# Scoring tokens against code words in quarters of 32, eight groups to a score bank, in a residual quantizer

## The chip, the cores and the metric

The kernel runs on one core of one Trainium2 chip. The metric is the device time of one execution in microseconds (us). Three runs of the kernel before gave 798.52, 801.80 and 803.55 us; their median, 801.8 us, is the time before.

The profile names the engines PE (TensorE, matmuls; PEld is its weight load), DVE (VectorE), ACT (ScalarE), POOL (GpSimd) and SP (SyncE, which issues transfers here).

## The reference

A small audio codec: a depthwise filter of three taps along time, SiLU, four stages of residual vector quantization with eight code words each, and a second depthwise filter over the sum of the chosen words.

```python
B, T, D, K = 2, 16000, 512, 3
Nq, C = 4, 8

z = zeros_like(x)
for i in range(K):
    z = z + xp[:, i:i+T, :] * dw_enc[i][None, None, :]
z = silu(z)
res, q = z, zeros_like(z)
for s in range(Nq):
    cb = codebooks[s]
    d2 = einsum("btd,btd->bt", res, res)[..., None] - 2.0 * einsum("btd,cd->btc", res, cb) + einsum("cd,cd->c", cb, cb)[None, None, :]
    idx = d2.argmin(-1)
    sel = cb[idx]
    q = q + sel
    res = res - sel
y = zeros_like(x)
for i in range(K):
    y = y + qp[:, i:i+T, :] * dw_dec[i][None, None, :]
return y
```

`xp` and `qp` are x and q with one row of zeros ahead of and behind each sequence. All arrays are bf16. The squared norm of the residual is part of each distance, so it has to be computed for every token and stage.

## The kernel before

**Layout.** The 32,000 tokens are 250 groups of 128: partition p holds 250 successive tokens, and group g is the token g of every partition. The 512 features are four blocks (index i) of 128, features on partitions. The groups are cut into 17 chunks (`SIZES`: 4, 12, fourteen of 16, 10). A chunk that is no multiple of four is padded, so the last one is worked on as 12.

**Front of a chunk** (`load`, `front`). The first two chunks come in as rows and are turned by TensorE; the others come through transposing transfers on SP's queue (L361), one for each group and two for the neighbours. Then for each feature block: three products with the taps on VectorE (L415); their sum, one addition by an accumulating transfer on POOL's queue (L421) and one on VectorE (L423), in the first two chunks both on VectorE; SiLU as exp (ScalarE, L427), plus one (VectorE, L431), log (ScalarE, L435), exp (ScalarE, L438), and the product with z (VectorE, L443), which writes the residual tile `RES`.

**RES.** One of three buffers, 128 x 4 blocks x 32 halves x 96 columns. A half is 64 tokens, with 16 columns of code words (times -2) ahead of it and 16 behind it. `code_columns` (L221, L222) writes these columns once in each buffer.

**A stage** (`stage`, four for each chunk). `score` fills a PSUM bank with up to `GB` = 6 groups: a matmul of the identity with `MASK` (L494) puts 0 on the diagonal and a huge negative number beside it; then, for each group, feature block and half of 64 tokens, a matmul (L499) has the 64 tokens as weights, and as moving operand the same 64 tokens with the code words that lie beside them as far as this stage needs: 80 columns in the first and last stage, 72 in the others. The diagonal of the 64 x 64 part is the squared norm; the mask lets a maximum over the row find it. `norm` (L507, VectorE) takes that maximum over 64 columns a group, `dots` (L510, VectorE) copies the eight products with code words. A chunk of 16 has three banks a stage, of 6, 5 and 5 groups; two banks exist. Six small instructions on VectorE (L527 to L554) make the one-hot choice, TensorE turns it (L564), ScalarE copies it out (L571).

Then the chosen words are subtracted from RES, for each feature block i and each pair of quarters of the chunk (j = 0 and 2). Blocks with i below `on_dve[s]` go over VectorE: TensorE puts the words in PSUM (L589, SEL) and VectorE adds (L604). The other blocks go over ScalarE: TensorE adds RES and words in PSUM (L610 and L589, NEW) and ScalarE copies back (L615). `ON_DVE` gives two blocks to VectorE in each of the three stages that subtract; its second row holds for the last chunk alone (`LAST` = 1). The last stage subtracts nothing.

**Output** (`finish`, `outputs`). The decoder's taps are multiplied into the code words at the start, so each output group is a sum of two matmuls on the turned one-hot choices (L640); ScalarE copies pairs of groups out (L646) into one of `YB` = 3 buffers, and SP stores four groups at a time.

**The order.** Nothing is placed by hand: `Plan` holds every step with an engine, a cost (hold and delay), what it needs and a due time, plays the engines forward with these costs, and at each point gives a free engine the ready step with the earliest due. The order that comes out is the program's. Buffers are counted as slots in it (`ZB`, `TB`, `EB`, `LNB`, `YB`, three RES buffers, two score banks `psG`, three `psA`). `LEAD`, `STAGE`, `LATE` and `SPREAD` set the dues in units of `PERIOD`: a block of a chunk's front is due at its chunk's origin plus (i x SPREAD - LEAD) periods, stage s at s x STAGE, the output at 3 x STAGE + LATE. Where the plan finds TensorE little used in its last 3.4 us, `warm` puts in a matmul that nobody reads (L316), to keep the engine's clock up.

Of the kernel before, what the change touches and what calls it, by code (L numbers as in the profile page):

```python
# [10 lines left out]
BF16 = mybir.dt.bfloat16  # L11
F32 = mybir.dt.float32
ALU = mybir.AluOpType
ACT = mybir.ActivationFunctionType
AX = mybir.AxisListType
# [2 lines left out]

GC = 16
J = 4  # L20
GB = 6
HT = 64
LC = 16

SIZES = [4, 12] + [16] * 14 + [10]


ON_DVE = ((2, 2, 2), (2, 3, 3))
LAST = 1

WARM = 0.5

DMA_ADDS = 1
DMA_MORE = 0

ZB, TB, EB, LNB, YB = 4, 5, 2, 1, 3
PERIOD, LEAD, STAGE, LATE, SPREAD = 48, 0.6, 0.7, 1.2, 0.2
FAR = -3.3e38


# [80 lines left out]
def kernel(  # L121
# [8 lines left out]
    nc = tc.nc  # L130
    P = nc.NUM_PARTITIONS
    B, T, D = x.shape
    K = dw_enc.shape[0]
    Nq, C, _ = codebooks.shape
    KT = D // P
    S = B * T // P
    NC = Nq * C
    HB = P // B
    assert K == 3 and D % P == 0 and B * T % P == 0 and P % B == 0 and J * NC == P and Nq * C == 32


    xf = x.flatten_outer_dims()
# [2 lines left out]
    const = ctx.enter_context(tc.tile_pool(name="const", bufs=1))  # L145
# [8 lines left out]
    psG = ctx.enter_context(tc.tile_pool(name="psG", bufs=2, space=bass.MemoryType.PSUM))  # L154
# [27 lines left out]
    for i in range(KT):  # L182
# [1 line left out]
    nc.vector.tensor_copy(WENC, psw[:, 0:4 * KT].rearrange("p (i k) -> p i k", k=4)[:, :, 0:K])  # L184

    free = {"RES": [], "KEY": [], "OH": []}
    plan = Plan({"XT": 2, "Z": ZB, "T": TB, "E": EB, "LN": LNB, "Y": YB, "psG": 2, "psA": 3, "RES": 3, "KEY": 3,
                 "OH": 3})

    RESB = []  # L190
    for n in range(3):
        t = const.tile([P, KT, 2 * GC, NC + HT], BF16, name=f"RES{n}")
        RESB.append(t)
        free["RES"].append(t)

# [1 line left out]

    xv = xf.rearrange("(p g) d -> p g d", g=S)
    G, G2 = chunks[0]["G"], chunks[0]["G"] + chunks[1]["G"]
    XR = RESB[2].rearrange("p k h c -> p (k h c)")[:, 0:(G2 + 2) * D].rearrange("p (g d) -> p g d", d=D)  # L200
    nc.vector.memset(XR[0:1, 0, :], 0.0)
    nc.vector.memset(XR[HB:HB + 1, 0, :], 0.0)
    nc.sync.dma_start(out=XR[:, 1:G + 2, :], in_=xv[:, 0:G + 1, :])
# [14 lines left out]
                                scalar2=None, op0=ALU.mult)  # L218

    def code_columns(t):  # L220
        nc.vector.tensor_copy(t[:, :, :, 0:LC], CBT[:, :, :, 0:LC].to_broadcast([P, KT, 2 * GC, LC]))  # L221
        nc.vector.tensor_copy(t[:, :, :, LC + HT:], CBT[:, :, :, LC:].to_broadcast([P, KT, 2 * GC, LC]))  # L222


    GPOS = const.tile([P, NC], BF16, name="GPOS")
# [16 lines left out]
        nc.vector.tensor_copy(GPOS, psg[:, 0, 0:NC])  # L242


    MASK = const.tile([P, GB, HT], BF16, name="MASK")

    def mask():
        for h in range(2):
            for r in range(GB):
                nc.vector.tensor_scalar(out=MASK[h * HT:(h + 1) * HT, r, :], in0=IDENT[h * HT:(h + 1) * HT, h * HT:(h + 1) * HT],  # L250
                                        scalar1=-1.0, scalar2=-FAR, op0=ALU.add, op1=ALU.mult)


    CBN = [const.tile([P, D], BF16, name=f"CBN{s}") for s in range(Nq - 1)]
# [41 lines left out]
    early = -4.0 * PERIOD  # L296
    words_in = plan.add("WORDS", 3.5, 3.5, [], early, lambda: None)
    codes = [plan.add("DVE", 0.3, 0.5, [words_in], early, code_words)]
    codes[0] = plan.add("DVE", 1.2, 1.4, codes, early + 2.0, lambda: code_columns(RESB[0]))
    scored = [plan.add("DVE", 2.4, 2.6, [], early + 1.0, mask), plan.add("DVE", 1.9, 2.1, [words_in], early + 1.0, code_norms)]  # L300
    preset = [plan.add("DVE", 0.8, 1.0, [], early + 2.0 if n == 0 else 0.1 * PERIOD, lambda n=n: presets(n)) for n in range(3)]
    words = plan.add("DVE", 1.0, 1.2, [words_in], early + 3.0, stage_words)
    codes.append(plan.add("DVE", 1.2, 1.4, [codes[0]], 0.1 * PERIOD, lambda: code_columns(RESB[1])))
    decoder = []
    for n, name in enumerate(PARTS):
        t = plan.add("DVE", 0.2, 6.0, [], (0.3 + 0.02 * n) * PERIOD, lambda name=name: taps_of(name))
# [14 lines left out]
    def load_rows(st, org):  # L321
        G, g0 = st["G"], st["g0"]
        moved = []

        def room():
            st["XT"] = xpool.tile([P, KT, GC + 2, P], BF16, name="XT")

        def turn(i):
            pst = psA.tile([P, 2, 512], F32, name="ps_x", tag="psa")
            st["ps", i] = pst.rearrange("p b n -> p (b n)").bitcast(BF16)  # L330
            for n in range(G + 2):
                nc.tensor.transpose(st["ps", i][:, n * P:(n + 1) * P], XR[:, g0 + n, i * P:(i + 1) * P], IDENT)

        def move(i):
            src = st["ps", i][:, 0:(G + 2) * P].rearrange("p (n t) -> p n t", t=P)
            if i % 2:
                nc.vector.tensor_copy(st["XT"][:, i, 0:G + 2, :], src)
            else:
                nc.scalar.activation(st["XT"][:, i, 0:G + 2, :], src, ACT.Copy)

        rows = plan.add("ROWS", 0.1 + 0.9 * G, 0.1 + 0.9 * G, [], early + org, room, take=("XT",))
        for i in range(KT):
            t = plan.add("PE", 0.12 * (G + 2), 0.12 * (G + 2) + 0.2, [rows], early + org, lambda i=i: turn(i),
                         take=("psA",))
            moved.append(plan.add(("ACT", "DVE")[i % 2], (0.11, 0.07)[i % 2] * (G + 2), (0.11, 0.07)[i % 2] * (G + 2) + 0.2, [t],
                                  early + org, lambda i=i: move(i), give=("psA",)))
        st["loaded"] = moved
        if g0:
            codes.append(plan.add("DVE", 1.2, 1.4, moved + codes[0:1], early + org + 1.0, lambda: code_columns(RESB[2])))

    def load(st, org):
        g0, G, GP = st["g0"], st["G"], st["GP"]
# [33 lines left out]
    def front(st, org):  # L386
# [14 lines left out]
        def places(t):  # L401
            return t[:, 0:G, :].rearrange("p (j m) t -> p j m t", m=MB)

        def halves(t):
            return t[:, 0:G, :].rearrange("p n (h t) -> p (n h) t", t=HT)

        def block(i):
            u = {}
# [31 lines left out]
            def silu():  # L440
                if i == 0:
                    st["RES"] = free["RES"].pop(0)
                nc.vector.tensor_tensor(out=st["RES"][:, i, 0:2 * G, LC:LC + HT], in0=halves(u["Z"]), in1=halves(u["E"]),  # L443
                                        op=ALU.mult)

            due = org + (i * SPREAD - LEAD) * PERIOD

# [26 lines left out]
    def stage(st, s, due):  # L474
# [4 lines left out]
        u = {}  # L479
        seen, maxima = [], []  # L480


        lo, hi = (min(C * s, LC), LC + HT) if C * s < LC else (LC, LC + HT + C * (s + 1) - LC)
        own = LC - lo
        pick = 0 if C * s < LC else hi - lo - C

        def score(q, m):
            RES = st["RES"]
            if q == 0:
                u["TR"] = small.tile([P, GC], BF16, name="TR")  # L490
                u["PR"] = small.tile([P, GC, C], BF16, name="PR")
            PS = pending.pop() if pending else psG.tile([P, 512], F32, name="PS")
            V = u["V", q] = PS[:, 0:m * (hi - lo)].rearrange("p (r c) -> p r c", r=m)
            nc.tensor.matmul(V[:, :, own:own + HT], lhsT=IDENT, rhs=MASK[:, 0:m, :], start=True, stop=False, skip_group_check=True)  # L494
            for r in range(m):
                for i in range(KT):
                    for h in range(2):
                        half = RES[:, i, 2 * (q + r) + h, :]
                        nc.tensor.matmul(V[h * HT:(h + 1) * HT, r, :], lhsT=half[:, LC:LC + HT], rhs=half[:, lo:hi],  # L499
                                         start=False, stop=(i == KT - 1), skip_group_check=True)  # L500
            if s == Nq - 1 and q + m == G:
                free["RES"].append(RES)
            if not scored[2:]:
                scored.append(None)

        def norm(q, m):
            nc.vector.tensor_reduce(out=u["TR"][:, q:q + m], in_=u["V", q][:, :, own:own + HT], axis=AX.X, op=ALU.max)  # L507

        def dots(q, m):
            nc.vector.tensor_copy(u["PR"][:, q:q + m, :], u["V", q][:, :, pick:pick + C])  # L510

        banks = -(-G // GB)
        q = 0
        for n in range(banks):
            m = -(-(G - q) // (banks - n))
            needs = [st["new"][i, j] for i in range(KT) for j in range(q // MB, (q + m - 1) // MB + 1)]
            needs += scored[0:2] + ([codes[st["n"]]] if st["n"] < 3 else [])
            t = plan.add("PE", 0.05 + 0.25 * m, 0.25 + 0.25 * m, needs, due, lambda q=q, m=m: score(q, m), take=("psG",),
                         give=("RES",) if s == Nq - 1 and q + m == G else (), use=0.7)
            seen.append(t)  # L520
            maxima.append(plan.add("DVE", 0.07 + 0.065 * m, 0.2 + 0.065 * m, [t], due, lambda q=q, m=m: norm(q, m)))
            maxima.append(plan.add("DVE", 0.06 + 0.01 * m, 0.2, [maxima[-1]], due, lambda q=q, m=m: dots(q, m), give=("psG",)))
            q += m

# [65 lines left out]
                             skip_group_check=True)  # L590

        def tokens(i, j, count):
            return st["RES"][:, i, 2 * j * MB:2 * (j + count) * MB, LC:LC + HT]

        def pair(i, j):
            return tokens(i, j, 2).rearrange("p (h m) t -> p h m t", h=2)

        def chosen(i, j):
            u["SEL", i, j] = psA.tile([P, 2, 512], F32, name="SEL", tag="psa")
# [2 lines left out]

        def subtract(i, j):
            nc.vector.tensor_tensor(out=pair(i, j), in0=pair(i, j), op=ALU.add,  # L604
                                    in1=u["SEL", i, j][:, :, 0:W].rearrange("p h (m t) -> p h m t", t=HT))

        def rest(i, j):
            NEW = u["NEW", i, j] = psA.tile([P, 2, 512], F32, name="NEW", tag="psa")
# [3 lines left out]
                select(NEW[:, h, 0:W], i, j + h, False)  # L612

        def keep(i, j):
            nc.scalar.activation(pair(i, j), u["NEW", i, j][:, :, 0:W].rearrange("p h (m t) -> p h m t", t=HT), ACT.Copy)  # L615

        due += 0.01 * PERIOD
        for j in range(0, J, 2):
# [122 lines left out]
```

## Time and profile before

| | |
|---|---|
| median of three runs | 801.8 us |
| the profiled execution, its own time | 801.33 us |
| its span, first to last instruction | 799.5 us |
| busy: DVE, ACT, PE, PEld, POOL | 733.6, 677.3, 654.2, 321.9, 62.8 us |
| granted TensorE clock, mean | 0.935 |
| L604 subtraction on VectorE | 208 instructions, 228.7 us |
| L615 subtraction on ScalarE | 200 instructions, 187.8 us |
| L499 score matmuls | 8064 instructions |
| L507 maxima on VectorE | 188 instructions, 94.4 us |
| L427, L435, L438 on ScalarE | 68 instructions each, 122.3, 122.3 and 122.4 us |
| L646 output copies on ScalarE | 126 instructions, 124.9 us |

In the profile L with a number is a line of the kernel; `out<-in` are tile names; a matmul's `128*64` is the weights' rows and columns. A row's mean is from an instruction's start to its end, and on one engine the next instruction may start before that end; the busy time of an engine counts overlapped time once. Idle time ahead of a group is given with what ended it. The busy time of PE holds pipelined matmuls whose ends are modelled.

### The profile page before, as it was taken

Reading aid. Unit: us, or ns where it says so; the run is one execution under the profiler, and the core shown is the slowest. Engines: PE = TensorE matmul, PEld = TensorE weight load, DVE = VectorE, ACT = ScalarE, POOL = GpSimd, SP = SyncE. Lnnn points to the kernel's source line nnn. Section 1 sums busy time; section 2 is a strip of 40 time slices with the busy share of each in tenths; the row PEclk is TensorE's granted clock in tenths of the full one; section 3 lists DMA queues with packets and bytes.
Section 4 is the critical chain, followed back from the end, with each engine's and each line's share of the span. In section 5 each row is a group of like instructions: output and inputs, shape, how many; then the busy total and the mean of one; then the engine's idle time right before and its main releaser. Section 6 shows DMA issues by size and latency. Waiting matters only on the chain.

```text
span 799.5 us, 23767 instructions
## 1 busy us (share of the span) xinstructions
PE 654.2 (82%) x10454; PEld 321.9 (40%) x10454; DVE 733.6 (92%) x1494; ACT 677.3 (85%) x603; POOL 62.8 (8%) x77
## 2 busy tenths in 40 slices
PE   1585878888888888878888798988888888889996
PEld 1333344433434443533444354444344443534443
DVE  5899799999999999999999999999999999968772
ACT  1567949799799998999998999989989998996666
POOL 0202010100001000000010100010000111000000
PEclk9987889999999998998999998999989999979999
DMA  7408595568676676799683997659767745120224
GB/s 185 81 16 147 110 146 104 97 130 167 129 132 154 116 156 134 121 186 192 133 148 67 216 143 158 121 102 206 163 136 147 142 89 146 33 88 3 107 107 184
DMA packets 162816, 102.77 MB, mean 129 GB/s; under 512 B 146201, under 2 KB 146586, under 8 KB 162586
## 3 DMA queue, kind: packets, MB, share of 16 engines
q1 hardware_dynamic: 153252, 69.77, 39.6%
q0 software_dynamic: 9312, 31.37, 22.5%
q8 instruction: 81, 1.33, 0.7%
q14 instruction: 21, 0.17, 0.1%
q10 hardware_dynamic: 150, 0.13, 0.1%
HBM read 2.92 MB, written 32.77 MB: 45 GB/s over the span
## 4 chain that ended last, share of the span: by engine, by line
DVE 55%; ACT 18%; PE 18%; DMA 5%; issue 2%; SPq 0%; POOL 0%; ACTq 0%; DVEq 0%
DVE RES L604 17%; DVE T L415 7%; DVE Z L423 6%; DVE TR L507 6%; DVE RES L443 5%; ACT YSB L646 5%; PE PS L499 4%; PE NEW L610 4%; ACT RES L615 4%; DVE Z L415 3%; ACT E L427 3%; ACT LN L435 3%; DVE E L431 3%; PE Y L640 3%; ACT E L438 3%
## 5 line engine op out<-in xcount | busy, mean ns | idle before, releaser
L604 DVE TENSOR_TENSOR RES<-RES,SEL 128x1024 bf16<-128x1024 bf16 (+2 forms) x208 | 228.7, 1128 | 12.5 <-PE SEL L589 12.2
L615 ACT ACTIVATE RES<-NEW 128x1024 bf16<-128x1024 f32 (+2 forms) x200 | 187.8, 976 | 58.1 <-PE NEW L589 54.4
L499 PE MATMUL PS<-RES 128*64 128x80 bf16 (+1 forms) x8064 | 185.1, 206 | 23.3 <-DVE RES L443 18.9
L499 PEld LDWEIGHTS <-RES 128*64 128x64 bf16 x8064 | 161.2, 117 | 67.1 <-issue 32.2
L610 PE MATMUL NEW<-RES,IDENT 128*128 128x512 bf16 (+2 forms) x400 | 124.9, 397 | 39.9 <-ACT RES L615 14.6
L427 ACT ACTIVATE E<-Z 128x2048 bf16<-128x2048 bf16 (+2 forms) x68 | 122.3, 1802 | 22.4 <-DVE Z L423 22.3
L435 ACT ACTIVATE LN<-E 128x2048 f32<-128x2048 bf16 (+2 forms) x68 | 122.3, 1798 | 10.4 <-DVE E L431 10.1
L646 ACT ACTIVATE YSB<-Y 128x1024 bf16<-128x1024 f32 (+1 forms) x126 | 124.9, 1035 | 5.9 <-PE Y L640 4.8
L438 ACT ACTIVATE E<-LN 128x2048 bf16<-128x2048 f32 (+2 forms) x68 | 122.4, 1800 | 0.3
L507 DVE TENSOR_REDUCE TR<-PS 128x6 bf16<-128x384 f32 (+2 forms) x188 | 94.4, 505 | 23.6 <-PE PS L499 23.6
L421 POOL DMA_DIRECT2D Z<-T x60 | 56.0, 933 | 607.9 <-DVE T L415 105.6
L589 PEld LDWEIGHTS <-CBN 32*128 32x128 bf16 x816 | 37.7, 92 | 158.4 <-issue 153.8
L589 PE MATMUL SEL<-OHT,CBN 32*128 32x512 bf16 (+2 forms) x416 | 73.2, 382 | 33.7 <-ACT OHT L571 13.6
L415 DVE TENSOR_SCALAR T<-XT,WENC 128x2048 bf16<-128x2048 bf16 (+2 forms) x136 | 94.4, 702 | 0.0
L640 PE MATMUL Y<-A,OHT 128*128 128x512 bf16 x249 | 82.5, 385 | 7.4 <-ACT YSB L646 6.1
L316 PE MATMUL PS<-CB,IDENT 128*128 128x512 bf16 x269 | 85.5, 435 | 2.8 <-DVE PR L510 2.8
L423 DVE TENSOR_TENSOR Z<-Z,T 128x2048 bf16<-128x2048 bf16 (+2 forms) x76 | 82.6, 1086 | 1.0 <-DMA Z<-T 1.0
L589 PE MATMUL NEW<-OHT,CBN 32*128 32x512 bf16 (+2 forms) x400 | 80.0, 396 | 0.0
L443 DVE TENSOR_TENSOR RES<-Z,E 128x2048 bf16<-128x2048 bf16 (+2 forms) x68 | 77.0, 1133 | 0.6 <-ACT E L438 0.6
L494 PE MATMUL PS<-MASK,IDENT 128*128 128x384 bf16 (+2 forms) x188 | 61.7, 328 | 10.2 <-DVE PR L510 9.8
L610 PEld LDWEIGHTS <-IDENT 128*128 128x128 bf16 x400 | 30.6, 100 | 84.9 <-issue 78.8
L640 PEld LDWEIGHTS <-OHT 128*128 128x128 bf16 x373 | 32.3, 99 | 40.9 <-issue 12.7
(74 smaller groups left out, 453.1 us busy)
## 6 DMA issues: line engine op xcount, KB each, us to landing
out_dram<-YSB SPq DMA_DIRECT2D x61, 512.0 KB, 3.2
Z<-T POOLq DMA_DIRECT2D x56, 512.0 KB, 5.7
XT<-in_x_dram SPq DMA_TRANSPOSE x263, 4.4
RES<-in_x_dram SPq DMA_DIRECT2D x1, 1536.0 KB, 10.0
Z<-T POOLq DMA_DIRECT2D x4, 384.0 KB, 6.0
RES<-in_x_dram SPq DMA_DIRECT2D x1, 640.0 KB, 6.3
out_dram<-YSB SPq DMA_DIRECT2D x1, 384.0 KB
out_dram<-YSB SPq DMA_DIRECT2D x1, 256.0 KB, 4.4
```

The lines of the kernel that those rows point to most:

```text
L415: nc.vector.tensor_scalar(out=places(u[name]), in0=taps(i, k), scalar1=WENC[:, i, k:k + 1], scalar2=None, op0=ALU.mult)
L427: nc.scalar.activation(u["E"][:, 0:G, :], u["Z"][:, 0:G, :], ACT.Exp, scale=-1.0)
L435: nc.scalar.activation(u["LN"][:, 0:G, :], u["E"][:, 0:G, :], ACT.Ln)
L438: nc.scalar.activation(u["E"][:, 0:G, :], u["LN"][:, 0:G, :], ACT.Exp, scale=-1.0)
L499: nc.tensor.matmul(V[h * HT:(h + 1) * HT, r, :], lhsT=half[:, LC:LC + HT], rhs=half[:, lo:hi], start=False, stop=(i == KT - 1), skip_group ...
L507: nc.vector.tensor_reduce(out=u["TR"][:, q:q + m], in_=u["V", q][:, :, own:own + HT], axis=AX.X, op=ALU.max)
L589: nc.tensor.matmul(ps, lhsT=CBN[s][rows, i * P:(i + 1) * P], rhs=u["OHT"][rows, 0:MB, :], start=start, stop=True, skip_group_check=True)
L604: nc.vector.tensor_tensor(out=pair(i, j), in0=pair(i, j), op=ALU.add, in1=u["SEL", i, j][:, :, 0:W].rearrange("p h (m t) -> p h m t", t=HT))
L610: nc.tensor.matmul(NEW[:, h, 0:W], lhsT=IDENT, rhs=tokens(i, j + h, 1), start=True, stop=False, skip_group_check=True)
L615: nc.scalar.activation(pair(i, j), u["NEW", i, j][:, :, 0:W].rearrange("p h (m t) -> p h m t", t=HT), ACT.Copy)
L640: nc.tensor.matmul(Y[:, h, :], lhsT=lhs(), rhs=rhs, start=(a == 0), stop=(a == len(terms) - 1))
L646: nc.scalar.activation(u["YSB"][:, k:k + n, :], u[k][:, 0:n, :], ACT.Copy)
```

## The change

- RES is 128 x 4 blocks x 65 quarters x 32 columns: 64 quarters of 32 tokens without gaps, and one last block with all 32 code words, written by one copy for each buffer instead of two.
- `score` has four matmuls, one for each quarter of a group's 128 tokens, for each feature block: 32 tokens as weights, and a moving operand of two stretches, the same 32 tokens and the block of all code words, 64 columns in every stage. `n::LAST_Q - n` picks blocks n and `LAST_Q`. The mask is 32 wide for each group, and `norm` takes its maximum over 32 columns.
- `GB` is 8: a bank holds eight groups of 64 columns, and a chunk of 16 has two banks a stage.
- L443, L604 and L615 write and read RES without gaps.
- `SIZES` is 4, 8, thirteen of 16, 12, 12, 6: 18 chunks, the last worked on as 8. `ON_DVE`'s second row holds for the last three and is (3, 2, 3) instead of (2, 3, 3).
- One more buffer for Z and for E, one fewer for the output; `LEAD`, `LATE` and `SPREAD` and the plan's costs of scores, maxima and code columns are other numbers.
- The mask is made by four instructions and a copy instead of twelve instructions.

```diff
-GB = 6
-HT = 64
-LC = 16
-SIZES = [4, 12] + [16] * 14 + [10]
-ON_DVE = ((2, 2, 2), (2, 3, 3))
-LAST = 1
+GB = 8
+QT = 32
+RB = 3
+SIZES = [4, 8] + [16] * 13 + [12, 12, 6]
+ON_DVE = ((2, 2, 2), (3, 2, 3))
+LAST = 3
...
-ZB, TB, EB, LNB, YB = 4, 5, 2, 1, 3
-PERIOD, LEAD, STAGE, LATE, SPREAD = 48, 0.6, 0.7, 1.2, 0.2
+ZB, TB, EB, LNB, YB = 5, 5, 3, 1, 2
+PERIOD, LEAD, STAGE, LATE, SPREAD = 48, 0, 0.7, 0.9, 0.1
...
+    LAST_Q = GC * P // QT
     RESB = []
-    for n in range(3):
-        t = const.tile([P, KT, 2 * GC, NC + HT], BF16, name=f"RES{n}")
+    for n in range(RB):
+        t = const.tile([P, KT, LAST_Q + 1, QT], BF16, name=f"RES{n}")
...
     def code_columns(t):
-        nc.vector.tensor_copy(t[:, :, :, 0:LC], CBT[:, :, :, 0:LC].to_broadcast([P, KT, 2 * GC, LC]))
-        nc.vector.tensor_copy(t[:, :, :, LC + HT:], CBT[:, :, :, LC:].to_broadcast([P, KT, 2 * GC, LC]))
+        nc.vector.tensor_copy(t[:, :, LAST_Q:, :], CBT)
...
     def mask():
-        for h in range(2):
-            for r in range(GB):
-                nc.vector.tensor_scalar(out=MASK[h * HT:(h + 1) * HT, r, :], in0=IDENT[h * HT:(h + 1) * HT, h * HT:(h + 1) * HT],
-                                        scalar1=-1.0, scalar2=-FAR, op0=ALU.add, op1=ALU.mult)
+        for h in range(P // QT):
+            own = slice(h * QT, (h + 1) * QT)
+            nc.vector.tensor_scalar(out=MASK[own, 0, :], in0=IDENT[own, own], scalar1=-1.0, scalar2=-FAR, op0=ALU.add, op1=ALU.mult)
+        nc.vector.tensor_copy(MASK[:, 1:, :], MASK[:, 0:1, :].to_broadcast([P, GB - 1, QT]))
...
-                nc.vector.tensor_tensor(out=st["RES"][:, i, 0:2 * G, LC:LC + HT], in0=halves(u["Z"]), in1=halves(u["E"]),
-                                        op=ALU.mult)
+                nc.vector.tensor_tensor(out=st["RES"][:, i, 0:G * P // QT, :].rearrange("p q t -> p (q t)"), in0=flat(u["Z"]),
+                                        in1=flat(u["E"]), op=ALU.mult)
...
-        lo, hi = (min(C * s, LC), LC + HT) if C * s < LC else (LC, LC + HT + C * (s + 1) - LC)
-        own = LC - lo
-        pick = 0 if C * s < LC else hi - lo - C
...
-            V = u["V", q] = PS[:, 0:m * (hi - lo)].rearrange("p (r c) -> p r c", r=m)
-            nc.tensor.matmul(V[:, :, own:own + HT], lhsT=IDENT, rhs=MASK[:, 0:m, :], start=True, stop=False, skip_group_check=True)
+            V = u["V", q] = PS[:, 0:m * 2 * QT].rearrange("p (r c) -> p r c", r=m)
+            nc.tensor.matmul(V[:, :, 0:QT], lhsT=IDENT, rhs=MASK[:, 0:m, :], start=True, stop=False, skip_group_check=True)
             for r in range(m):
                 for i in range(KT):
-                    for h in range(2):
-                        half = RES[:, i, 2 * (q + r) + h, :]
-                        nc.tensor.matmul(V[h * HT:(h + 1) * HT, r, :], lhsT=half[:, LC:LC + HT], rhs=half[:, lo:hi],
+                    for h in range(P // QT):
+                        n = (q + r) * P // QT + h
+                        nc.tensor.matmul(V[h * QT:(h + 1) * QT, r, :], lhsT=RES[:, i, n, :], rhs=RES[:, i, n::LAST_Q - n, :],
                                          start=False, stop=(i == KT - 1), skip_group_check=True)
...
-            nc.vector.tensor_reduce(out=u["TR"][:, q:q + m], in_=u["V", q][:, :, own:own + HT], axis=AX.X, op=ALU.max)
+            nc.vector.tensor_reduce(out=u["TR"][:, q:q + m], in_=u["V", q][:, :, 0:QT], axis=AX.X, op=ALU.max)
...
-            nc.vector.tensor_copy(u["PR"][:, q:q + m, :], u["V", q][:, :, pick:pick + C])
+            nc.vector.tensor_copy(u["PR"][:, q:q + m, :], u["V", q][:, :, QT + C * s:QT + C * s + C])
...
-            t = plan.add("PE", 0.05 + 0.25 * m, 0.25 + 0.25 * m, needs, due, lambda q=q, m=m: score(q, m), take=("psG",),
+            t = plan.add("PE", 0.1 + 0.19 * m, 0.3 + 0.19 * m, needs, due, lambda q=q, m=m: score(q, m), take=("psG",),
                          give=("RES",) if s == Nq - 1 and q + m == G else (), use=0.7)
             seen.append(t)
-            maxima.append(plan.add("DVE", 0.07 + 0.065 * m, 0.2 + 0.065 * m, [t], due, lambda q=q, m=m: norm(q, m)))
+            maxima.append(plan.add("DVE", 0.1 + 0.033 * m, 0.23 + 0.033 * m, [t], due, lambda q=q, m=m: norm(q, m)))
...
         def tokens(i, j, count):
-            return st["RES"][:, i, 2 * j * MB:2 * (j + count) * MB, LC:LC + HT]
+            return st["RES"][:, i, j * W // QT:(j + count) * W // QT, :].rearrange("p q t -> p (q t)")
```

The plan's costs of `code_columns` go from 1.2 to 0.2, and `pair`, `subtract` and `keep` drop the reshaping that the gaps needed.

## The prediction

> **What bounds the kernel now.** I read the page's chain of waits first, for the engine that sets the end, and then the busy time by stretches. The chain:
>
> ```profile
> DVE 55%; ACT 18%; PE 18%; DMA 5%; issue 2%; SPq 0%; POOL 0%; ACTq 0%; DVEq 0%
> ```
>
> VectorE (DVE) holds over half of it. The stretches tell where (length, then busy us with instruction counts of PE, PEld, DVE, ACT, POOL; granted clock; DMA):
>
> ```profile
> 0.00:100.00 100.00, 59.35 (x576) 29.84 (x577) 81.17 (x217) 60.51 (x59) 9.65 (x17) 0.89 0.54 108
> 100.00:160.00 60.00, 49.96 (x909) 25.75 (x908) 57.81 (x122) 43.19 (x40) 5.57 (x7) 0.89 0.68 116
> 160.00:653.00 493.00, 418.44 (x6970) 204.95 (x6970) 484.91 (x920) 463.87 (x392) 42.56 (x49) 0.95 0.75 144
> 700.00:799.50 99.50, 86.33 (x1308) 41.05 (x1307) 63.58 (x144) 69.59 (x77) 0.00 (x0) 0.94 0.24 97
> ```
>
> The window 160 to 653 runs from the first L443 of the fifth chunk to that of the sixteenth, eleven chunks of 16 groups: one period is 493/11 = 44.8 us. VectorE is busy 484.9/11 = 44.1 us of it (98%), ScalarE (ACT) 42.2 (94%), TensorE (PE) 38.0, of which the warming matmuls of L316, 39.3 us in this window, are 3.6. So VectorE bounds the middle, with ScalarE only 1.9 us behind. In the last 99.5 us neither is full: there the chain of stages of the last chunks decides.
>
> Then the groups of instructions, shapes kept apart (count | busy us, mean ns | idle before):
>
> ```profile
> L507 DVE TENSOR_REDUCE TR<-PS 128x5 bf16<-128x320 f32 x112 | 53.7, 481 | 7.7 <-PE PS L499 7.6
> L507 DVE TENSOR_REDUCE TR<-PS 128x6 bf16<-128x384 f32 x72 | 39.4, 547 | 14.8 <-PE PS L499 14.8
> L507 DVE TENSOR_REDUCE TR<-PS 128x4 bf16<-128x256 f32 x4 | 1.7, 416 | 1.2 <-PE PS L499 1.2
> L537 DVE TENSOR_REDUCE M<-D 128x16 bf16<-128x128 bf16 x56 | 15.4, 275 | 0.1
> L537 DVE TENSOR_REDUCE M<-D 128x12 bf16<-128x96 bf16 x8 | 2.0, 249 | 0.1
> L443 DVE TENSOR_TENSOR RES<-Z,E 128x2048 bf16<-128x2048 bf16 x56 | 67.9, 1212 | 0.6 <-ACT E L438 0.6
> L423 DVE TENSOR_TENSOR Z<-Z,T 128x2048 bf16<-128x2048 bf16 x56 | 67.9, 1212 | 1.0 <-DMA Z<-T 1.0
> ```
>
> L507 costs 65 ns per 64 elements. L537 costs 26 ns for 4 rows of 8, so the price goes by element, and short rows carry no surcharge.
>
> Means overlap their neighbours, so I price a step by start to next start, in VectorE's timeline (start, us):
>
> ```profile
> 505.33 0.54 DVE L507 TENSOR_REDUCE TR<-PS 128x6 bf16<-128x384 f32 x1
> 505.80 0.27 DVE L554 TENSOR_TENSOR OH<-KEY,M 128x128 bf16<-128x128 f32 x1
> 506.00 0.19 DVE L510 CAST PR<-PS 128x48 bf16<-128x48 f32 x1
> 506.12 0.67 DVE L431 TENSOR_SCALAR E<-E 128x2048 bf16<-128x2048 bf16 x1
> ...
> 508.51 0.48 DVE L507 TENSOR_REDUCE TR<-PS 128x5 bf16<-128x320 f32 x1
> 508.91 0.73 DVE L415 TENSOR_SCALAR T<-XT,WENC 128x2048 bf16<-128x2048 bf16 x1
> 509.57 0.18 DVE L510 CAST PR<-PS 128x40 bf16<-128x40 f32 x1
> 509.68 0.47 DVE L507 TENSOR_REDUCE TR<-PS 128x5 bf16<-128x320 f32 x1
> ```
>
> Steps: reduce 0.47 (six groups) and 0.40 (five); copy of the dots 0.12 and 0.11. The score matmuls' pace is in the weight loads' timeline; the banks at 503 and 513 move 80 columns, those at 519 and 521 move 72:
>
> ```profile
> 503.17 0.93 PEld L499 LDWEIGHTS <-RES 128*64 128x64 bf16 x48 [0.37 <-issue]
> 513.03 0.79 PEld L499 LDWEIGHTS <-RES 128*64 128x64 bf16 x40
> 519.71 0.86 PEld L499 LDWEIGHTS <-RES 128*64 128x64 bf16 x48 [0.37 <-issue]
> 521.32 0.73 PEld L499 LDWEIGHTS <-RES 128*64 128x64 bf16 x40 [0.16 <-issue]
> ```
>
> Less one load (0.11), 0.82/47 = 17.4 ns per matmul at 80 columns, 0.75/47 = 16.0 at 72: the ratio is 1.09, that of the columns 1.11. The two halves run as one pair, 34.9 and 32.0 ns, and the columns set the pair.
>
> **The change, part by part.** *Norms and dots.* Of 16 groups a stage now has three banks (6, 5, 5): 0.47 + 2×0.40 + 0.12 + 2×0.11 = 1.61 us. After: two banks of 8, each a reduce over 8×32 = 256 elements, 0.33 by the same line, and a copy of 64, 0.14: 0.94 us. Four stages save 2.7 us per period. The means instead of the steps would give 3.3; if the copies cost double, 2.1. All of it is on VectorE, so its period falls to 41.4.
>
> *Residuals without gaps.* L443 writes with gaps and takes 1212 ns as gap-free L423 does: nothing. L604 and L615 have no gap-free twin of their own; bounds 0 to −0.03 us on 12 instructions each, taken as 0.
>
> *Scores.* Four quarters of 32 replace two halves of 64, each over 32 + 32 columns: twice the matmuls and loads, 64 columns each. If four quarters run together as two halves do, the rows give 32.0 − 8×0.36 = 29.1 ns per round, 64 rounds a stage: 1.86 us against 2.14 now. Masks: two at 0.21 for three at about 0.25. TensorE then needs 38.0 − 3.6 − 4×0.6 = 32 us per period without warming. From the other side: the shown feed is two instructions in 16.0 ns, 8 ns each; if that is the limit, 512 instructions take 4.1 us a stage, 1.6 more after the masks, and TensorE needs 41. I take the first, as the pace follows columns in every bank above, and keep the second as a rival. A second stretch in the moving operand has no row here; it goes with these ends. TensorE is off the bound by 10 us in the one case and by none in the other.
>
> The Trainium skill speaks against it: by "TensorE: Matmul & The Clock Gate", section "Wait — 56ns, not 53.3ns?", starts of matmuls never come closer than about 25 ns, an estimated 6.4 us for a stage's 256. Across two column tiles the 16.0 ns above contradict it.
>
> *What is late next.* ScalarE's 42.2 us per period are untouched and now above VectorE's 41.4. VectorE keeps 98% busy today with a second engine at 94%; with both within 2% each will at times wait for the other. I take 98% for the new leader: 42.2/0.98 = 43.0 us. Ends: 42.2 (never waits) and 44.4 (95%). From 160 to 700 there are 12 periods: 12×1.8 = 22 us off (31 to 5). Between 100 and 160 ScalarE has slack (72%) and VectorE 96%, so 1.3 periods give the full 2.7, less a little: 3. Together 25.
>
> *Start.* Three pairs of code-column copies (0.66 and 0.68 us) become three small ones (128x128: 0.18), the mask 5 instructions for 12: 4.5 us less on VectorE, which is idle 19 us in the first 100; on the path 1.
>
> *One more chunk* (4, 8, 13×16, 12, 12, 6). Its fixed parts: ScalarE 12 activations, by 0.63 us at 512 and 1.93 at 2048 elements 0.19 each that does not go by size; VectorE some 48 instructions, by L415's 0.35 and 0.74 us 0.21 each, 0.08 of it overlapped: 2 and 6 us. The period is set by ScalarE, so +4 between them. Its two more transposing loads and one store on SP's queue lie under a DMA share of 0.75.
>
> *Tail.* The last three chunks give one more block to L604 in two stages: VectorE +6 us net, ScalarE −5, both covered by VectorE's 36 idle us after 700. The last chunk is padded to 8 groups, not 12. Today the four stages behind the last L443 at 722.5 take 77 us; a third less of an eight-group chain's own work, against more chunks beside it, gives −6 (−12 to +6, since the front is no longer due ahead). Fewer output buffers (two): L646 waited 0.9 us in all for a store; 0 to +2. More buffers for E and Z only relax waits; taken as 0.
>
> Sum on the profiled execution's 801.33 us (span 799.5): −25 −1 +4 −6 = 773.3; with the median of the runs 0.5 above that execution, **774 us**. Ends: 801.3 − 34 − 2 + 2 − 12 = 755, and, with half the tail's gain, 801.3 − 8 + 4 − 3 = 794.
>
> **The rivals.**
> *ScalarE and the order eat the gain.* Both engines near 42 us, fed through each other (exp, add one, log, exp, multiply) and in the order the plan writes from guessed costs: the period stays 44 to 44.8, 801.3 − 3 + 4 − 3 = 799 (794 to 806). For it: ScalarE is 94% busy already. Against: its longest idle, 58.1 us before L615, ends with TensorE's NEW, and TensorE gets less to do.
> *TensorE's feed becomes the bound; slower.* Place: L499. Price: 8 ns per instruction, TensorE at 41 us. In no stretch above is it over 87% busy; at 88% the period is 41/0.88 = 46.6, 13.3 periods of +1.8: 801 + 24 = 825. It decides from about 6.5 ns an instruction (3.3 us a stage, TensorE 37.8 us, 88% of the 43.0), and the kernel gets slower from 7.2. For it: no row shows a faster feed. Against: the paces above are those of columns.
> *The quarters run one after another.* Then a round of 29.1 ns is paid for each matmul: 256 a stage, 7.4 us, 4×(7.4 + 0.42 − 2.14 − 0.74) = +20 on 34.4, and 54/0.88 = 62 us a period: about 1030 us. Against: two halves share a round now. The page's floor, named above, would act in the same way.
> *Quarters do nothing for VectorE*: a 256-element reduce at 416 ns is in the rows, so I give it nothing.
>
> **How the numbers follow.** Forecast, 755 to 794: 0.72. Better (ScalarE never waits, tail shorter than bounded): 0.05. Gain eaten: 0.10. Feed-bound: 0.11. One after another: 0.02. Range 755 to 806, which leaves out 0.05 below and 0.13 above. One per cent, about what a measurement tells here, is 8 us, so 793.8 and 809.8: faster 0.72 + 0.05 = 0.77; same 0.10; slower 0.13.
>
> **What would show it.** L507 at 416 ns over 128x256 and L510 at about 0.21, two of each per stage; a full bank of 128 score loads in about 1.0 us (2.0 or more for the feed rival, 3.7 for quarters in turn); in the middle ScalarE above 96% busy, VectorE below it, a period of 43; after 700 less idle time. I am wrong if the period stays at 44.8 with all three engines under 95%, or if waits of L507 for L499 grow from today's 23.6 us.

## The result and the profile after

The changed kernel takes 894.9 us (median of four runs, 880.4 to 898.6) against 802.7 us. The ratio is 1.105, with an interval of 1.090 to 1.119: it is slower by a tenth. The profiled execution took 892.0 us, its span is 890.2. Ratios, here and below, compare undisturbed runs alone (here 880.4 and 892.0 us), and where an experiment has none, only one of its two runs was undisturbed.

The page of the changed kernel, its chain by engine and the group at the head of its list (as before: count | busy us, mean ns | idle before and what ended it):

```profile
PE 38%; ACT 24%; DVE 16%; issue 15%; DMA 6%; SPq 1%; POOL 0%; DVEq 0%; ACTq 0%
...
L497 PE MATMUL PS<-RES 128*32 128x64 bf16 x16128 | 192.3, 206 | 125.1 <-issue 103.6
```

VectorE held 55% of the chain and holds 16%; TensorE has 38%, and 15% is "issue", time in which an engine waited for nothing that the profile shows. The list puts 103.6 us of such idle time before the score matmuls. Before the change, L499 had no such entry: its 23.3 us of idle time ended with work of VectorE and ScalarE.

```profile
L499 PE MATMUL PS<-RES 128*64 128x80 bf16 (+1 forms) x8064 | 185.1, 206 | 23.3 <-DVE RES L443 18.9 <-DVE RES L604 3.7 <-ACT RES L615 0.6
```

Busy time by stretch, from the fifth chunk's first L445 to the fifteenth's, ten chunks of 16 groups, and after it (length, then PE, PEld, DVE, ACT, POOL, clock, DMA):

```profile
167.00:680.00 513.00, 381.36 (x11207) 191.37 (x11262) 418.68 (x757) 414.24 (x348) 38.02 (x41) 0.88 0.77 126
680.00:890.00 210.00, 168.87 (x4791) 82.97 (x4806) 160.32 (x357) 159.88 (x170) 12.50 (x16) 0.93 0.40 101
```

A period is 51.3 us, up from 44.8. VectorE needs 41.9 of it, 2.2 less than before, so the relief is there. But it is busy 82% only, ScalarE 81%, TensorE 74%: no engine is full.

VectorE's own groups, shapes apart, and what its maxima waited for:

```profile
L505 DVE TENSOR_REDUCE TR<-PS 128x8 bf16<-128x256 f32 x112 | 47.0, 420 | 106.4 <-PE PS L497 104.1 <-issue 2.3
L508 DVE CAST PR<-PS 128x64 bf16<-128x64 f32 x112 | 24.1, 216 | 0.0
```

The maxima over all shapes wait 111.1 us for the scores (23.6 before). One such wait, in TensorE's timeline (start, us, instruction, and in brackets the idle time before it):

```profile
346.37 0.28 PE L491 MATMUL PS<-MASK,IDENT 128*128 128x256 bf16 x1
346.58 0.79 PE L497 MATMUL PS<-RES 128*32 128x64 bf16 x76
351.66 0.89 PE L497 MATMUL PS<-RES 128*32 128x64 bf16 x52 [4.29 <-issue]
```

A bank breaks off after 76 of its 128 matmuls and goes on 4.3 us later. In the chain over the same stretch the gap is a piece of its own:

```profile
346.65 0.72 PE PS L497 x76
347.37 4.29 issue
351.66 0.89 PE PS L497 x48
```

The matmul that ends the gap waits for no semaphore. What happened in between is in the view of the DMA queues: in the tenth of a microsecond from 348.9 the queue of instructions started one packet, of 16 KB (number of packets, MB, share of the 16 engines in this stretch):

```profile
q8 instruction: 1, 0.02, 67.8%
```

67.8% of 16 engines over 0.1 us is 1.08 us, so it had landed by 350.1, and TensorE went on 1.6 us later. I counted the same picture over the whole trace: starts of TensorE more than 0.5 us behind the one before, on an instruction without a semaphore wait, 1.0 to 2.2 us behind the end of such a packet. The changed kernel has 70, 124 us in all, and the packet's end lies 1.4 us ahead of them in the median. The kernel before has 4, 2.2 us in all. The bounds of 1.0 and 2.2 us do not make this picture: all 35 gaps over 1.5 us without a semaphore wait end 1.2 to 1.6 us behind a packet's end, and the kernel before has no such gap.

The pages count 145 such packets after and 81 before:

```profile
q8 instruction: 145, 2.38, 1.1%
```

```profile
q8 instruction: 81, 1.33, 0.7%
```

2.38 MB over the 37,060 matmuls and weight loads of TensorE is 64 bytes each, so a packet holds 256. One bank of eight groups is 128 weight loads and 128 matmuls: a whole packet. The 35 long gaps stand whole packets apart: from one to the next there are 255 to 2298 of these instructions, each time a multiple of 256 or up to 6 fewer (the few may be instructions without a record; that is not shown). So a bank breaks off where one packet's instructions end.

### The profile page after: what moved, and what is told of

Its sections match the earlier page's. It is cut to its first block, busy times and chain, and to the rows that moved or that the text cites. A ratio compares the mean times of both kernels' runs of the same rounds, so it can differ in the third digit from the quotient of the medians.

```text
span 890.2 us, 39931 instructions
## 1 busy us (share of the span) xinstructions
PE 658.9 (74%) x18481; PEld 330.3 (37%) x18579; DVE 709.0 (80%) x1440; ACT 676.5 (76%) x623; POOL 65.4 (7%) x81
## 3 DMA queue, kind: packets, MB, share of 16 engines
q1 hardware_dynamic: 156516, 70.03, 43.2%
q8 instruction: 145, 2.38, 1.1%
## 4 chain that ended last, share of the span: by engine, by line
PE 38%; ACT 24%; DVE 16%; issue 15%; DMA 6%; SPq 1%; POOL 0%; DVEq 0%; ACTq 0%
PE PS L497 15%; ACT YSB L644 6%; ACT RES L613 6%; PE NEW L608 6%; PE Y L638 5%; DVE RES L602 5%; ACT E L440 5%; ACT LN L437 4%; PE NEW L587 4%; PE SEL L587 3%; DMA out_dram<-YSB 2%; ACT E L429 2%; DVE T L417 2%; PE PS L318 2%; DVE RES L445 2%
## 5 line engine op out<-in xcount | busy, mean ns | idle before, releaser
L497 PE MATMUL PS<-RES 128*32 128x64 bf16 x16128 | 192.3, 206 | 125.1 <-issue 103.6
L602 DVE TENSOR_TENSOR RES<-RES,SEL 128x1024 bf16<-128x1024 bf16 (+3 forms) x228 | 235.8, 1069 | 33.7 <-PE SEL L587 32.6
L613 ACT ACTIVATE RES<-NEW 128x1024 bf16<-128x1024 f32 (+3 forms) x204 | 184.7, 942 | 81.0 <-PE NEW L587 68.8
L497 PEld LDWEIGHTS <-RES 128*32 128x32 bf16 x16128 | 165.7, 102 | 163.2 <-issue 132.0
L644 ACT ACTIVATE YSB<-Y 128x1024 bf16<-128x1024 f32 (+1 forms) x126 | 127.2, 1033 | 43.6 <-PE Y L638 27.4
L505 DVE TENSOR_REDUCE TR<-PS 128x8 bf16<-128x256 f32 (+2 forms) x132 | 53.8, 408 | 113.5 <-PE PS L497 111.1
L608 PE MATMUL NEW<-RES,IDENT 128*128 128x512 bf16 (+3 forms) x371 | 113.9, 383 | 27.8 <-ACT RES L613 9.5
L429 ACT ACTIVATE E<-Z 128x2048 bf16<-128x2048 bf16 (+3 forms) x72 | 122.7, 1712 | 4.8 <-DVE Z L425 4.8
L437 ACT ACTIVATE LN<-E 128x2048 f32<-128x2048 bf16 (+3 forms) x72 | 123.4, 1714 | 3.0 <-DVE E L433 2.7
L440 ACT ACTIVATE E<-LN 128x2048 bf16<-128x2048 f32 (+3 forms) x72 | 123.3, 1713 | 0.2
L417 DVE TENSOR_SCALAR T<-XT,WENC 128x2048 bf16<-128x2048 bf16 (+3 forms) x144 | 96.0, 677 | 3.0 <-DMA Z<-T 3.0
L425 DVE TENSOR_TENSOR Z<-Z,T 128x2048 bf16<-128x2048 bf16 (+3 forms) x80 | 81.9, 1026 | 0.5 <-DMA Z<-T 0.5
L445 DVE TENSOR_TENSOR RES<-Z,E 128x2048 bf16<-128x2048 bf16 (+3 forms) x72 | 77.9, 1083 | 4.9 <-ACT E L440 4.5
```

Of the source, the lines that this page charges most:

```text
L417: nc.vector.tensor_scalar(out=places(u[name]), in0=taps(i, k), scalar1=WENC[:, i, k:k + 1], scalar2=None, op0=ALU.mult)
L429: nc.scalar.activation(u["E"][:, 0:G, :], u["Z"][:, 0:G, :], ACT.Exp, scale=-1.0)
L437: nc.scalar.activation(u["LN"][:, 0:G, :], u["E"][:, 0:G, :], ACT.Ln)
L440: nc.scalar.activation(u["E"][:, 0:G, :], u["LN"][:, 0:G, :], ACT.Exp, scale=-1.0)
L497: nc.tensor.matmul(V[h * QT:(h + 1) * QT, r, :], lhsT=RES[:, i, n, :], rhs=RES[:, i, n::LAST_Q - n, :], start=False, stop=(i == KT - 1), s ...
L608: nc.tensor.matmul(NEW[:, h, 0:W], lhsT=IDENT, rhs=tokens(i, j + h, 1), start=True, stop=False, skip_group_check=True)
```

## The experiments

Three theories. **A, supply:** TensorE runs through its instructions faster than they are brought. **B, order:** the new sizes, dues and buffers make a worse order. **C, quarters:** four tiles side by side, or the second stretch, are slow in the array.

**Half the feature blocks.** Two of the four blocks are scored.

```diff
-                for i in range(KT):
+                for i in range(KT // 2):
...
```

> The changed kernel with scores over two of the four feature blocks (the other two are left out), in the same order: 8064 score matmuls instead of 16128. Theory A, supply: TensorE runs out of instructions, because a bank of 8 groups is 257 pairs of load and matmul and the next block of instructions lands too late. Then the idle time before the score matmuls that ends with nothing the profile shows (103.6 us) falls under 25 us and the time to 770 to 815 us. Theory B, order: the new sizes, dues and buffers make a worse order; the time stays at 870 to 900. Theory C, quarters: four tiles side by side or the second stretch are slow in themselves; half of that is gone, 830 to 850.

Measured: 786.0 us, ratio 0.984 [0.977, 0.992]. Idle time before the scores that nothing ends: 12.5 us, not 103.6; 82 instruction packets; VectorE 703.5 us busy. (A bank of eight groups is 129 pairs of load and matmul with its mask, not the 257 of the expectation.)

```profile
L497 PE MATMUL PS<-RES 128*32 128x64 bf16 x8064 | 96.9, 203 | 22.1 <-issue 12.5
```

The order is the changed kernel's, so B falls as the cause of the loss. C was expected to leave it at 830 or more. The granted clock is no rival either: its mean was 0.935 before and 0.887 after the change, and 0.889 in this run.

**More instructions in the kernel before.**

```diff
                         nc.tensor.matmul(V[h * HT:(h + 1) * HT, r, :], lhsT=half[:, LC:LC + HT], rhs=half[:, lo:hi],
                                          start=False, stop=(i == KT - 1), skip_group_check=True)
+                        nc.tensor.matmul(PS[h * HT:h * HT + 33, 511:512], lhsT=half[:, LC:LC + 33], rhs=half[:, LC:LC + 1],
+                                         start=False, stop=(i == KT - 1), skip_group_check=True)
```

> The kernel before with one more matmul behind each score matmul, of one column with 33 columns of weights, into a PSUM column that nobody reads: 16128 score pairs instead of 8064, the order and all work of VectorE and ScalarE as before. Theory A, supply: the idle time of TensorE before score matmuls that nothing ends rises from about 0 to 60 us or more, instruction blocks rise from 81 to about 145, and the time to 850 to 900 us. Theories B and C: no new wait of that kind; the small matmuls cost array time alone, 800 to 835 us.

Measured: 893.1 and 911.9 us, 144 packets. The time is near the range of A, but the idle time that nothing ends is 28.0 us before the scores and the small matmuls together, not the 60 that A was to bring. The run decides nothing, because the small matmuls are not small. TensorE's timeline in a bank:

```profile
250.37 0.21 PE L499 MATMUL PS<-RES 128*64 128x80 bf16 x2
250.41 0.18 PE L501 MATMUL PS<-RES 128*33 128x1 bf16 x2
250.44 0.21 PE L499 MATMUL PS<-RES 128*64 128x80 bf16 x2
250.47 0.18 PE L501 MATMUL PS<-RES 128*33 128x1 bf16 x2
```

A pair of one-column matmuls lengthens the round from 35 to about 68 ns, and over 72 columns from 32 to 64. Over 4032 rounds that is some 130 us of TensorE, more than the 41 us of stalls behind a packet. The Trainium skill says as much, in "TensorEngine Tiling (Array Packing)", section "Instruction Overhead": a matmul over one column takes as long as one over 60. This run agrees: the one-column pair takes about 32 ns, as long as the pair over 72 columns.

**Same columns, half the matmuls.** The clean form: one matmul of 128 columns for two groups in place of two of 64. The scores use the weights of every other group only.

```diff
-            for r in range(m):
+            for r in range(0, m, 2):
...
-                        nc.tensor.matmul(V[h * QT:(h + 1) * QT, r, :], lhsT=RES[:, i, n, :], rhs=RES[:, i, n::LAST_Q - n, :],
+                        nc.tensor.matmul(V[h * QT:(h + 1) * QT, r:r + 2, :], lhsT=RES[:, i, n, :],
+                                         rhs=RES[:, i, (q + r) * P // QT:(q + r) * P // QT + 4, :],
```

> The changed kernel with one score matmul of 128 columns for two groups in place of two of 64 (weights of the first group of each two alone, so the scores are not the reference's): 8064 instead of 16128 pairs of load and matmul, about the same columns through the array (55 ns a round for two groups against two rounds of 31.5). Theory A, supply by count of instructions: as with two of the four feature blocks, 780 to 805 us, instruction blocks near 82, and idle time before score matmuls that nothing ends under 25 us. Theory C, array time of quarters: no gain, 870 to 895 us.

Measured: 780.3 us, ratio 0.975 [0.964, 0.985]. The score group of this kernel, and its busy time from the fifth chunk's first L445 to the fifteenth's:

```profile
L497 PE MATMUL PS<-RES 128*32 128x128 bf16 x8064 | 149.1, 228 | 30.8 <-DVE RES L445 19.2 <-issue 10.1 <-ACT RES L614 1.3
```

```profile
154.00:589.00 435.00, 344.14 (x6278) 162.79 (x6327) 414.76 (x758) 410.51 (x346) 39.65 (x41) 0.95 0.79 147
```

As many columns go through four quarters as in the changed kernel, in the same order, and 10.1 us of idle time that nothing ends are left. The period is 43.5 us with VectorE at 95% and ScalarE at 94%. So neither the array nor the order takes the time: the number of instructions per bank does. This form computes something else and is no replacement. (It also lacks the second stretch; the changed kernel's own unbroken banks clear that, below.)

**Fewer loads.** The changed kernel; chunks from the fifth on work on the tiles of the third and fourth.

```diff
+            if st["n"] >= 4:
+                st["XT"] = chunks[2 + st["n"] % 2]["XT"]
+                return
```

> The changed kernel without the transposing loads of x from the fifth chunk on; these chunks work on the data of the third and fourth. All instructions of TensorE, VectorE and ScalarE stay. Theory A, supply, in the form that an instruction block comes late because it queues behind these loads on the DMA engines: stalls before score matmuls that nothing ends fall from 103.6 to under 50 us in total, their longest from 5.6 to under 2.5 us, and the time to 800 to 850 us. Theories B and C: 870 to 895 us, as VectorE's work and the order are the same.

Measured: 870.2 us (862.5 and 877.8), outside the 800 to 850 of A in this form. Queue q1 takes 13.8% of the DMA engines instead of 43.2%, and the idle time before the scores falls from 103.6 us to 80.2, the longest from 5.6 to 4.7. By the count described above, stalls go from 124 to 106 us and their median from 1.5 to 1.0 us. Time, stalls and longest stall all miss what was expected. A packet queued behind loads is then the smaller part: most of the stall time is there with these loads gone (the additions on POOL's queue and the stores remain). What the loads seem to add is in the longest stalls: 9 are over 3 us in the changed kernel, 36.2 us in all, and 2 here, 8.2 us.

**The new plan under the kernel before, the old one under the quarters.** Each kernel with the other's sizes, `ON_DVE`, `LAST`, buffers and dues.

```diff
-ZB, TB, EB, LNB, YB = 4, 5, 2, 1, 3
-PERIOD, LEAD, STAGE, LATE, SPREAD = 48, 0.6, 0.7, 1.2, 0.2
+ZB, TB, EB, LNB, YB = 5, 5, 3, 1, 2
+PERIOD, LEAD, STAGE, LATE, SPREAD = 48, 0, 0.7, 0.9, 0.1
...
```

> The kernel before (halves of 64, banks of six) with the changed kernel's chunk sizes, blocks to VectorE, buffers and due times. Theory B, order: most of the loss is here, 860 us or more. Theories A and C: 785 to 815 us, and no idle time before score matmuls that nothing ends.

> The changed kernel's quarters, banks of eight and residuals without gaps with the sizes, dues, buffers and blocks to VectorE of the kernel before (the rows of the first two chunks get a tile of their own, as RES is now too small for them). Theory A: the stalls stay, 104 us or so of idle time that nothing ends, and the time is 865 to 895 us, 1 to 2 per cent under the changed kernel as the new plan cost the kernel before 1.4 per cent. Theory B, order: 800 us or less.

Measured: the kernel before with the new plan 809.6 us, 1.014 [1.000, 1.028]; the quarters with the old plan 899.5 us, 1.123 [1.117, 1.130], with 88.9 us of idle time before the scores that nothing ends. The second missed: the old plan does not help the quarters. B explains 11 us (0 to 22) under the halves, and nothing of the loss under the quarters.

**Pacing.** If the rate in a bank is what hurts, the same instructions spread out should stall less. A bank's scores become pieces of two groups, and the plan puts a piece on TensorE only if 256 instructions or fewer fall into 2.6 us of its own costs. The plan's costs of the scores are other numbers too.

```diff
+PIECE, BLOCK, BLOCK_US = 2, 256, 2.6
...
+                            if tasks[n][9] > 8 and sum(c for _, c in issued) + tasks[n][9] > BLOCK:
+                                heapq.heappush(events, (max(now + 0.02, issued[0][0] + BLOCK_US + 0.01), -1))
+                                passed.append((due, n))
+                                continue
```

> The changed kernel with the same instructions, but a bank's scores cut into pieces of two groups (64 instructions) and a plan that puts a piece on TensorE only if no more than 256 instructions fall into 2.6 us by its costs, so that other matmuls come between pieces. Theory A, supply by rate: the stalls fall to under 50 us and the time to 800 to 850 us. If the stalls are due to the total count and not to the rate in a bank, or to the quarters themselves, the time stays at 870 to 900 us.

> The paced pieces of the run before this one with the sizes, dues, buffers and blocks to VectorE of the kernel before. Theory A: stalls as low as in the paced run, and 10 us less from the older plan: 785 to 840 us. Theory C: 860 us or more.

Measured: 861.9 us, 1.076 [1.068, 1.085], with 47.3 us of that idle time; with the old plan 841.4 us, 1.051 [1.038, 1.064], with 54.2. Both keep all 16,128 score matmuls, and the idle time falls from 103.6 to 47.3 us with the new plan and from 88.9 to 54.2 with the old one: the rate counts, not the total alone. The first missed its range of times, and the second is 1.4 us above its own. Three more, all on the old plan: pieces of one group with 160 and with 192 instructions, and pieces of two with a rule that only prefers other matmuls and issues the piece where there are none.

> The paced kernel with the older plan, in pieces of one group and with no more than 160 instructions in 2.6 us of the plan instead of 256. Theory A, supply by rate: fewer stalls than at 256, under 45 us of idle time that nothing ends before score matmuls against 54; the time is 800 to 835 us, if what the plan itself leaves idle does not grow. If the stalls are not due to the rate, they stay near 54 us.

> The same with 192 instructions in 2.6 us: stalls and time between those at 160 and those at 256, 805 to 840 us.

> Pieces of two groups, the older plan, and a softer rule: above 192 instructions in 2.6 us of the plan another ready matmul goes first, but where there is none the piece is issued all the same, so that the rule itself leaves TensorE no idle time. Theory A, supply by rate: stalls between the 27.7 us at a hard 192 and the 103.6 of the changed kernel, and less waiting for what the plan holds back; 815 to 850 us. Under 800 us only if matmuls that could fill the gaps were at hand nearly everywhere.

Measured: 905.1 us (1.132), 846.3 us (832.9 and 859.8) and 901.7 us (1.128). All three have the stalls that were expected, and the first and the last miss their times by 50 us and more. The scores of the run at 160, and of the run at 192:

```profile
L510 PE MATMUL PS<-RES 128*32 128x64 bf16 x16128 | 242.0, 205 | 33.7 <-DVE RES L456 23.5 <-issue 9.9
```

```profile
L510 PE MATMUL PS<-RES 128*32 128x64 bf16 x16128 | 237.9, 201 | 51.8 <-issue 27.7 <-DVE RES L456 23.2
```

The stalls go as A says, 54.2, 27.7, 9.9 us with the limit falling, and 73.0 with the soft rule. The time does not follow: at 160 ScalarE waits 90.6 us for TensorE's NEW (68.8 in the changed kernel) and VectorE still 69.4 us for scores. As I read these waits, the plan holds the scores back by itself, and others wait for them; no run separates this. The soft rule does not hold back, and why it is as slow as 901.7 us with 73.0 us of stalls stays open. None of these is faster than the kernel before.

## Why the prediction was wrong, point by point

**VectorE's cost** was right. L507 was to take 416 ns over 256 elements and took 420 (as L505), the copy 0.21 and took 0.216. A period of 41.4 us of VectorE was forecast, 41.9 was measured, and 41.5 in the run with half the matmuls.

**The engine that is late next** came out nearly right where supply allows it: ScalarE was to lead with 42.2 us at 98%, a period of 43.0 us. The run with the same columns has 43.5, with VectorE at 95% and ScalarE, 41.1 us, at 94%. ScalarE does not lead, and neither reaches 98%, so part of the agreement is luck: less work and a lower share offset each other. Its 780 us are 6 above the forecast of 774.

**The pace of the scores** was nearly right inside an unbroken bank: 29.1 ns a round were worked out, 32 are measured. Such a bank of the changed kernel in the weight loads' timeline:

```profile
724.84 1.11 PEld L497 LDWEIGHTS <-RES 128*32 128x32 bf16 x128 [0.32 <-issue]
```

Less one load of 0.10 that is 1.01 us over 127, 8.0 ns a matmul and 32 a round. Four quarters with a second stretch do run side by side.

**The step that failed** is the choice under *Scores*: "I take the first, as the pace follows columns in every bank above, and keep the second as a rival." The rows showed the pace of banks of 96 instructions at most, each followed by long matmuls. They did not show what 256 in a row do, and I read them as the pace of any bank. What stands in its place: a bank takes 2.1 us from its first matmul's start to its last's in the mean (282.8 us over 132 banks, by the trace's records) instead of 1.0, and mostly because of gaps: 62 steps of over 0.5 us from one matmul of a bank to the next take 129 of these us, and 25 of the 112 full banks run at 8.1 ns a matmul. "TensorE is off the bound by 10 us" was true of its work, and no help: VectorE waits 111.1 us for it all the same.

**The rival "TensorE's feed becomes the bound"** named the place (L499, now L497) and the side, and had the wrong form. I priced a steady 8 ns per instruction, 825 us, from the fastest feed that a row showed. Over all banks the mean is near that, 8.8 ns (282.8 us over 15,996 steps of two instructions), but it is made of 4.0 ns for as long as there are instructions and of stops of up to 5.8 us, and the period became 51.3 us instead of that rival's 46.6. It had 0.11, and the range ended at 806. Its sign, waits of L507 for L499 above 23.6 us, came true.

**Smaller terms.** The plan's numbers were counted at +4 for the chunk and −6 for the tail; under the kernel before they cost +11 us [0 to 22]. The tail is shorter, 62 us behind the last L445 against 77, but under the kernel before the new plan makes the period 46.3 us (463 us over ten chunks) instead of 44.8. Two output buffers were to cost 0 to 2 us; L644 waits 10.5 for stores, 0.9 before.

**Open.** What starts a packet, how many instructions TensorE holds ahead, and why it goes on 1.4 us after a packet's end were not tried. That a packet starts late in the longest cases because of the transposing loads is supported only by the run with fewer of them: 2 stalls over 3 us instead of 9.

## What to carry to other kernels

Count the instructions in a burst, beside columns and elements. Here twice the matmuls for the same array work turned a saving of 2.5% (the run with half the matmuls) into a loss of 10%, and no engine's busy time shows it: look for idle time that ends with "issue" inside one group, and set it beside the packets of the instruction queue. A pace read from short bursts holds for short bursts.

## What the runs showed of the hardware

- TensorE's instructions come in packets of 16 KB, 256 instructions, and the long stalls stand at their borders. Stalls without a semaphore wait end 1.4 us (median) behind a packet's end: 124 us in the changed kernel, 2.2 before.
- Four column tiles of 32 with 64 columns run at 32 ns a round, eight instructions, as long as instructions are there: 4.0 ns an instruction.
- A pair of one-column matmuls with 33 columns of weights costs about 32 ns, as much as a pair over 72 columns (32.0).
